# A fused lightning-attention and SwiGLU kernel: the first tile's outputs inside the third tile, five half buffers for the activations, and another order of groups 4 and 5

## The chip, the cores and the metric

The kernel runs on one core of one Trainium2 chip. The time is device microseconds of one execution; the number for a kernel is the median of several runs. Beside these runs stands one execution taken with the hardware profiler, whose rows are used below. In that core PE (TensorE) multiplies matrices into PSUM, DVE (VectorE), ACT (ScalarE) and POOL (GpSimd) work on tensors, and SP (SyncE) issues transfers. Each engine works through its own instructions in order and waits for semaphores that others raise.

## The reference

Attention over q, k and v of shape (4 batches, 8 heads, 768 positions, 64), in blocks of 64 positions, with a running state per batch and head that decays with lambda; its result, laid out as 3072 tokens by 512, goes through a gated feed-forward network.

```python
for b in range(nb):
    intra = einsum('bhic,bhjc->bhij', qb, kb) * Dmask
    intra = einsum('bhij,bhjd->bhid', intra, vb)
    inter = einsum('bhid,bhde->bhie', qb * lam_pow, kv_state)
    out[:, :, sl] = intra + inter
    kv_state = lam_block * kv_state + einsum('bhsd,bhse->bhde', kb * rev_pow, vb)
...
g = x @ w_gate            # 512 -> 1536
h = g * sigmoid(g) * (x @ w_val)
return h @ w_out          # 1536 -> 512
```

## The kernel before, in words

**Groups and tiles.** A group g is 256 positions of one batch in all heads; there are 12. Two groups make a tile t of 512 tokens, the unit of the feed-forward part; there are six. Groups 0 to 5 (`g < NAT0`) and groups 6 to 11 use different layouts of the same computation.

**Attention of one group.** `load_group` (L243) issues the loads of k, q and v on SP: three transfers, or ten for groups 6 and up. `cast_scaled` (L255) casts k on ACT and scales and casts q on DVE (L260), then `dma_transpose` (L248) issues one transposing transfer on SP (L251), which makes `qkt`. `v_scale` (L235) makes `v_s` on POOL (L238). `upd_mm` (L382) multiplies k by v for the state, `upd_copy` (L404) copies that on ACT to `ups`, and `state` (L421 to L432) is a chain of adds and casts on POOL that gives the states `kvn` and `kv`. `scores` (L326, or L352 for groups 6 and up) multiplies q by k; the masks on DVE (L333, L357) are put in a list, `later`, and taken from it by `run_later`. `core_a` multiplies q by the states (L461) into two PSUM banks and lets ACT read one element (`guard`, L445); `core_b` adds the product of masked scores and v (L474) and then evicts both banks to `xt` (L486), on ACT unless `SPLIT` gives one to DVE. `ahead(g)` is update, state and scores; `attend(g)` is `core_a(g)`, the update and scores of g + 1, and `core_b(g)`, in one visit.

**Feed-forward part.** `ffn_gate` (L514) multiplies by a 128-wide slice of w_gate and ACT takes Silu (L518); `ffn_val` (L528) does the same with w_val and DVE multiplies the two into `h` (L531). Such a pair is a step; a tile has 12. Tile 1's steps are cut in two halves: `s1a` for its first group, `s1b` for its second. `ffn_out(t, b)` (L547) then multiplies 128 tokens of `h` by all of w_out in 12 matmuls, ACT evicts (L549) and issues the store (L550). A tile's `h` is one buffer of [128, 12, 4, 128]; there are two.

**Output weights.** w_out comes in six transfers of 512 KB on SP (`wo_piece`, L227) and is cast by POOL, one piece by ACT (`wo_cast`, L232).

**PSUM.** All eight banks are handed out in turn by `bank()`: whatever asks for a bank gets the one that was handed out eight requests before.

**Order.** The order is written by hand. `at(n, fn, ...)` puts a call behind step n; the loop at L768 emits each step, one or two waiting masks, and then the calls of that step. In tile 1 this puts group 5's loads and all six weight pieces on SP behind s1a[3], the casts and the transposition of group 5 behind s1b[3], `ahead(4)` behind s1b[6], and at the end of the tile, behind s1b[11]:

```python
    at(s1b[11], ffn_out, 0, 0)
    at(s1b[11], ahead, 5)
    at(s1b[11], run_later, 3)
    at(s1b[11], ffn_out, 0, 1)
    at(s1b[11], core_a, 5)
    at(s1b[11], ffn_out, 0, 2)
    at(s1b[11], core_b, 5)
```

From tile 2 on, `sn[n]` are the steps of a tile, each of which carries the four outputs of the tile before it behind steps 0, 3, 7 and 9, the casts and loads of two groups, and two `attend` calls.

Of the kernel before, what the change touches and what calls it, by code (L numbers as in the profile page):

```python
# [9 lines left out]
BF16 = mybir.dt.bfloat16  # L10
# [27 lines left out]
def _body(ctx, tc, nc, q, k, v, lam, moe_w_gate, moe_w_val, moe_w_out, out):  # L38
# [5 lines left out]
    DFF = moe_w_gate.shape[1]  # L44
    MC = DM // 128
    FC = DFF // 128
    NG = NBLK * B // 2
    M = BLK // 2

# [17 lines left out]
    vs_pool = ctx.enter_context(tc.tile_pool(name="vs", bufs=4))  # L67
    ssb_pool = ctx.enter_context(tc.tile_pool(name="ssb", bufs=2))
    xt_pool = ctx.enter_context(tc.tile_pool(name="xt", bufs=2))
    h_pool = ctx.enter_context(tc.tile_pool(name="h", bufs=2))  # L70
    sil_pool = ctx.enter_context(tc.tile_pool(name="sil", bufs=3))
    osb_pool = ctx.enter_context(tc.tile_pool(name="osb", bufs=3))
    kv_pool = ctx.enter_context(tc.tile_pool(name="kv", bufs=1))
# [234 lines left out]
    def scores(g, cs=(0, 1), warm=0):  # L308
        if g >= NAT0:
            scores_n(g)  # L310
            return
        tt = st[("qkt", g)]
        sp = {(c, h2): bank() for c in cs for h2 in range(2)}
        warm_into(sp[(cs[0], 0)], warm)
        if ("ssb", g) not in st:
            st[("ssb", g)] = ssb_pool.tile([128, 2, HP, 2, BLK], BF16, name="ssb", tag="ssb")
        ssb = st[("ssb", g)]
        for c in cs:
            for hi in range(2):
                for s in range(2):  # L320
                    for b2 in range(2):
                        for h2 in range(2):
                            hp = 2 * c + hi
                            dp = slice(h2 * 64, h2 * 64 + 64)
                            n = (hi * 2 + s) * BLK
                            nc.tensor.matmul(  # L326
                                sp[(c, h2)][b2 * M:b2 * M + M, n:n + BLK],
                                tt[dp, 0, s, hp, b2 * M:b2 * M + M],
                                tt[dp, 1, :, hp, b2 * M:b2 * M + M],
                                start=True, stop=True, skip_group_check=True)  # L330
            for h2 in range(2):
                def do_mask(c=c, h2=h2):
                    nc.vector.tensor_tensor(  # L333
                        out=ssb[:, h2, 2 * c:2 * c + 2].rearrange("p a s n -> p a (s n)"),
                        in0=sp[(c, h2)].rearrange("p (a x) -> p a x", a=2),
                        in1=bap(causal, [[0, 2], [1, 2 * BLK]]),
                        op=ALU.mult)
                later.append(do_mask)
# [179 lines left out]
        nc.scalar.activation(sil[:, 0:N], gp[:, 0:N], AF.Silu)  # L518

    def ffn_val(t, fc, b0=0, b1=B):  # L520
        if ("h", t) not in st:
            st[("h", t)] = h_pool.tile([128, FC, B, BLK], BF16, name="h", tag="h")
        h_sb, xt, sil = st[("h", t)], st[("xt", t)], st[("sil", t, fc, b0)]
        N = (b1 - b0) * BLK
        fs = slice(fc * 128, fc * 128 + 128)
        vp = bank()
        for mc in range(MC):
            nc.tensor.matmul(vp[:, 0:N], wv_sb[:, mc, fs],  # L528
                             xt[:, b0 // 2:b1 // 2, mc].rearrange("p g b n -> p g (b n)"),
                             start=(mc == 0), stop=(mc == MC - 1))  # L530
        nc.vector.tensor_tensor(out=h_sb[:, fc, b0:b1].rearrange("p b n -> p (b n)"),  # L531
                                in0=sil[:, 0:N], in1=vp[:, 0:N], op=ALU.mult)

    def ffn_fc(t, fc, b0=0, b1=B):
# [1 line left out]
        ffn_val(t, fc, b0, b1)  # L536

    def ffn_out(t, b, last=False):
        h_sb = st[("h", t)]
        osb = osb_pool.tile([128, DM], FP32, name="osb", tag="osb")  # L540
        row = groups[2 * t + b // 2][0] * S + (groups[2 * t + b // 2][1] * 2 + b % 2) * BLK
        halves = ((0, DM // 2, nc.scalar.copy, nc.scalar), (DM // 2, DM, nc.vector.tensor_copy, nc.sync)) \
            if last else ((0, DM, nc.scalar.copy, nc.scalar),)
        for c0, c1, fn, eng in halves:
            ps = bank()[:, 0:c1 - c0]
            for fc in range(FC):
                nc.tensor.matmul(ps, h_sb[:, fc, b], wo_sb[:, fc, c0:c1],  # L547
                                 start=(fc == 0), stop=(fc == FC - 1))
            fn(out=osb[:, c0:c1], in_=ps)  # L549
            eng.dma_start(out=bass.AP(tensor=out.tensor, offset=out.offset + row * DM + c0,  # L550
                                      ap=[[DM, 128], [1, c1 - c0]]),
                          in_=osb[:, c0:c1])
# [3 lines left out]
        upd(g)  # L556
        scores(g)

    def attend(g):
        run_later(len(later))  # L560
        core_a(g)
        if g + 1 < NG:
            upd_mm(g + 1)
            upd_copy(g + 1)
            scores(g + 1)
            late, later[:] = later[:], []
        core_b(g)
        if g + 1 < NG:
            later[:] = late
            state(g + 1)  # L570
# [106 lines left out]
    def at(n, fn, *a):  # L677
        plan.setdefault(n, []).append((fn, a))
# [31 lines left out]
    s1b = [step(1, fc, 2, 4) for fc in range(FC)]  # L710
    at(s1a[3], cast_scaled, 4)
    at(s1a[3], load_group, 5)
    for c in range(0, FC, 2):
        at(s1a[3], wo_piece, c, c + 2)
    at(s1a[7], scores, 3, (0,))
    at(s1a[7], run_later, 2)
    at(s1a[8], scores, 3, (1,))
# [4 lines left out]
    at(s1a[10], core_b, 3, SPLIT)  # L722
    at(s1a[10], v_scale, 4, nc.gpsimd)
    at(s1a[10], state, 3)
    at(s1b[3], cast_scaled, 5)
    at(s1b[3], load_group, 6)
    at(s1b[4], wo_cast)
    at(s1b[4], wo_cast)
    at(s1b[6], ahead, 4)
    at(s1b[6], run_later, 2)  # L730
    at(s1b[6], wo_cast)
    at(s1b[6], wo_cast)
    at(s1b[6], v_scale, 5, nc.gpsimd)
    at(s1b[8], wo_cast)
    at(s1b[9], core_a, 4)
    at(s1b[10], core_b, 4)
    at(s1b[10], wo_cast, ACTC)
    at(s1b[11], ffn_out, 0, 0)
    at(s1b[11], ahead, 5)
    at(s1b[11], run_later, 3)  # L740
    at(s1b[11], ffn_out, 0, 1)
    at(s1b[11], core_a, 5)
    at(s1b[11], ffn_out, 0, 2)
    at(s1b[11], core_b, 5)
    at(s1b[11], cast_scaled, 6)
    at(s1b[11], load_group, 7)
    at(s1b[11], v_scale, 6, nc.gpsimd)
    at(s1b[11], ffn_out, 0, 3)

    outs = [(1, b) for b in range(4)]  # L750
    for t in range(2, NG // 2):
        sn = [step(t, fc) for fc in range(FC)]
        if t == 2:
            at(sn[2], ahead, 6)
        for j, g in ((3 if t == 2 else 0, 2 * t + 3), (7 if t == 2 else 6, 2 * t + 4)):
            if g < NG:
                at(sn[j], cast_scaled, g)
                if g + 1 < NG:
                    at(sn[j], load_group, g + 1)
                at(sn[1 + j], v_scale, g, nc.gpsimd)  # L760
        if t + 1 < NG // 2:
            at(sn[6 if t == 2 else 4], attend, 2 * t + 2)
            at(sn[10], attend, 2 * t + 3)
        for n, o in zip((0, 3, 7, 9), outs):
            at(sn[n], ffn_out, *o)
        outs = [(t, b) for b in range(4)]

    for n, (t, fc, b0, b1) in enumerate(steps):  # L768
        if t >= 1 and t + 1 < NG // 2 and ("xt", t + 1) not in st:
# [5 lines left out]
            if fn in (attend, ahead):  # L775
                run_later(1)
    run_later(len(later))
    for t, b in outs:
        ffn_out(t, b, last=(b == 3))
# [1 line left out]
_INS = ['q', 'k', 'v', 'lam', 'moe_w_gate', 'moe_w_val', 'moe_w_out']  # L781
_OUTS = [((3072, 512), 'float32')]
# [25 lines left out]
```

## Time and profile before

| | |
|---|---|
| median of 5 runs | 228.57 us (228.2 to 229.05) |
| profiled execution | 228.97 us |
| its span on the core | 227.3 us |
| PE busy | 219.5 us (97%), 2443 matmuls |
| ACT, DVE, POOL busy | 108.0 (48%), 90.0 (40%), 88.0 us (39%) |
| gate, value and output matmuls (L514, L528, L547) | 76.6, 76.4, 65.8 us |
| moved by DMA | 39.70 MB |

The span runs from the first to the last recorded instruction; the execution's own time also holds what lies around it. In the profile's rows the order is start, duration, engine, line, operation, out<-in and count; a bracket gives the idle time of the engine before the row and what ended it. PE's rows are matmuls, PEld's the weight loads beside them, a q behind an engine's name marks what its sequencer issues. Matmuls overlap, so a row of PE lasts longer than the time until the next one starts; distances between starts are the safer reading.

### The profile page before, as it was taken

To read this page: it belongs to the slowest core of one execution; us is meant where nothing else is said; L and a number is where in the kernel's file an instruction comes from. 1 tells how busy PE (TensorE), PEld (TensorE's weight loads), DVE (VectorE), ACT (ScalarE), POOL (GpSimd) and SP (SyncE) were. 2 spreads that over 40 slices of the span, in tenths; PEclk is the share of its full clock that TensorE was granted. 3 is DMA by queue.
4 is the path that set the end of the run, shared out by engine and by line. 5 is a ranking of instruction groups with operands and counts; after the bars stand their busy time and mean duration, and the time that the engine had idled before them with its cause. 6 is when DMAs were issued, how large, how long until landed. Compare 5 with 4: busy or idle time off the path is not lost.

```text
span 227.3 us, 5902 instructions
## 1 busy us (share of the span) xinstructions
PE 219.5 (97%) x2443; PEld 118.3 (52%) x2443; DVE 90.0 (40%) x151; ACT 108.0 (48%) x211; POOL 88.0 (39%) x130
## 2 busy tenths in 40 slices
PE   8889999999998999999999999999999999999994
PEld 3556455878863444454544544544544444444443
DVE  2664357685834213545353362253242123222200
ACT  6888585754662446354454463453433423322221
POOL 6576737542595222978363092092150000000000
PEclk9999999999999999999999999999999999999999
DMA  6999999899997878887888748915101101101122
GB/s 194 345 360 382 367 356 311 201 260 276 386 189 191 224 164 200 197 185 186 217 191 194 191 95 192 242 31 138 49 3 48 46 3 46 46 0 46 49 92 92
DMA packets 88012, 39.70 MB, mean 175 GB/s; under 512 B 57650, under 2 KB 83506, under 8 KB 87986
## 3 DMA queue, kind: packets, MB, share of 16 engines
q1 hardware_dynamic: 83474, 32.64, 54.8%
q10 hardware_dynamic: 4512, 6.69, 8.3%
q8 instruction: 19, 0.31, 0.6%
q14 instruction: 7, 0.06, 0.1%
HBM read 28.31 MB, written 6.29 MB: 152 GB/s over the span
## 4 chain that ended last, share of the span: by engine, by line
PE 83%; DMA 5%; SPq 4%; POOL 4%; ACT 1%; issue 1%; DVE 0%; DVEq 0%; POOLq 0%
PE bank L547 27%; PE bank L514 25%; PE bank L528 24%; DMA woraw<-in_moe_w_out_dram 3%; SPq L99 3%; DMA kraw<-in_k_dram 2%; PE bank L474 2%; POOL wo_sb L232 2%; PE bank L461 2%; PE bank L382 1%; PE bank L352 1%; POOL v_s L238 1%; PE bank L289 1%; PE bank L326 1%; SPq L227 1%
## 5 line engine op out<-in xcount | busy, mean ns | idle before, releaser
L531 DVE TENSOR_TENSOR h<-sil,bank 128x512 bf16<-128x512 bf16 (+1 forms) x87 | 51.4, 594 | 105.9 <-PE bank L528 86.7
L514 PE MATMUL bank<-xt,wg_sb 128*128 128x512 bf16 (+1 forms) x348 | 76.6, 343 | 0.0
L528 PE MATMUL bank<-xt,wv_sb 128*128 128x512 bf16 (+1 forms) x348 | 76.4, 342 | 0.0
L547 PE MATMUL bank<-wo_sb,h 128*128 128x512 bf16 (+1 forms) x300 | 65.8, 371 | 1.3 <-POOL wo_sb L232 1.3
L518 ACT ACTIVATE sil<-bank 128x512 bf16<-128x512 f32 (+1 forms) x87 | 45.9, 527 | 43.9 <-PE bank L514 40.9
L528 PEld LDWEIGHTS <-wv_sb 128*128 128x128 bf16 x348 | 34.0, 98 | 28.3
L547 PEld LDWEIGHTS <-h 128*128 128x128 bf16 x300 | 29.1, 98 | 33.8 <-issue 1.5
L514 PEld LDWEIGHTS <-wg_sb 128*128 128x128 bf16 x348 | 32.4, 98 | 27.2 <-DVE xt L486 0.3
L549 ACT COPY osb<-bank 128x512 f32<-128x512 f32 (+1 forms) x24 | 13.9, 578 | 54.5 <-PE bank L547 52.4
L238 POOL TENSOR_TENSOR v_s<-v,dec 128x1024 bf16<-128x1024 f32 (+1 forms) x14 | 23.2, 1666 | 16.8 <-DMA v<-in_v_dram 9.4
L421 POOL TENSOR_TENSOR kvf<-kvs,ups 128x256 f32<-128x256 f32 x8 | 5.8, 726 | 42.0 <-ACT ups L404 42.0
L333 DVE TENSOR_TENSOR ssb<-bank,causal 128x512 bf16<-128x512 f32 x24 | 15.3, 683 | 4.4 <-PE bank L326 4.3
L486 ACT CAST xt<-bank 128x512 bf16<-128x512 f32 x21 | 12.8, 663 | 2.9 <-PE bank L474 2.4
L430 POOL CAST kvn<-kvf 64x256 bf16<-64x256 f32 x24 | 12.5, 519 | 1.5
L421 POOL TENSOR_TENSOR kvf<-kvf,ups 128x256 f32<-128x256 f32 x16 | 11.6, 725 | 0.6
L260 DVE TENSOR_TENSOR qk<-qraw,qdn 128x1024 bf16<-128x1024 f32 x6 | 8.1, 1350 | 6.5 <-DMA qraw<-in_q_dram 6.5
L404 ACT COPY ups<-bank 128x256 f32<-128x256 f32 (+1 forms) x24 | 9.5, 450 | 2.4 <-PE bank L382 1.4
L258 ACT CAST qk<-kraw 128x1024 bf16<-128x1024 f32 x9 | 9.4, 1040 | 0.6 <-DMA kraw<-in_k_dram 0.6
L357 DVE TENSOR_TENSOR ssb<-bank,causaln 128x512 bf16<-128x512 f32 x12 | 8.2, 687 | 1.2 <-PE bank L352 1.0
L232 POOL CAST wo_sb<-woraw 128x1024 bf16<-128x1024 f32 x5 | 5.2, 1043 | 6.8 <-DMA woraw<-in_moe_w_out_dram 6.8
L221 POOL CAST wv_sb<-wraw 128x1024 bf16<-128x1024 f32 (+1 forms) x6 | 5.8, 970 | 5.0 <-DMA wraw<-in_moe_w_val_dram 4.9
L474 PE MATMUL bank<-ssb,v_s 64*64 64x128 bf16 (+1 forms) x384 | 7.0, 208 | 0.5 <-ACT guard L445 0.5
(65 smaller groups left out, 118.6 us busy)
## 6 DMA issues: line engine op xcount, KB each, us to landing
out_dram<-osb ACTq DMA_DIRECT2D x23, 256.0 KB, 2.2
v<-in_v_dram SPq DMA_DIRECT2D x16, 256.0 KB, 4.4
woraw<-in_moe_w_out_dram SPq DMA_DIRECT2D x6, 512.0 KB, 7.6
kraw<-in_k_dram SPq DMA_DIRECT2D x24, 128.0 KB, 3.4
qraw<-in_q_dram SPq DMA_DIRECT2D x24, 128.0 KB, 4.2
wraw<-in_moe_w_gate_dram SPq DMA_DIRECT2D x5, 512.0 KB, 6.7
wraw<-in_moe_w_val_dram SPq DMA_DIRECT2D x5, 512.0 KB, 7.7
kraw<-in_k_dram SPq DMA_DIRECT2D x4, 512.0 KB, 6.7
```

The lines of the kernel that those rows point to most:

```text
L238: eng.tensor_tensor(out=st[("vs", g)][:, h0:h1], in0=st[("v", g)][:, h0:h1].rearrange("p h (s d) -> p h s d", s=2), in1=vfac(g, h0, h1), o ...
L333: nc.vector.tensor_tensor(out=ssb[:, h2, 2 * c:2 * c + 2].rearrange("p a s n -> p a (s n)"), in0=sp[(c, h2)].rearrange("p (a x) -> p a x", ...
L421: nc.gpsimd.tensor_tensor(out=o, in0=f, in1=u, op=ALU.add)
L430: nc.gpsimd.tensor_copy(out=o[64 - h2 * 64:128 - h2 * 64], in_=f[h2 * 64:h2 * 64 + 64])
L474: nc.tensor.matmul(op[r][h2 * 64:h2 * 64 + 64, cols(g, hp, s)], v_s[ps, 2 * hp + h2, s], ssb[ps, h2, hp * 2 + s] if g >= NAT0 else ssb[ps, ...
L486: fns[r](out=xt[:, g % 2, :, r].rearrange("p h (m s) -> p h s m", s=2) if g < NAT0 else xt[:, g % 2, :, :, r * M:r * M + M], in_=op[r].rea ...
L514: nc.tensor.matmul(gp[:, 0:N], wg_sb[:, mc, fs], xt[:, b0 // 2:b1 // 2, mc].rearrange("p g b n -> p g (b n)"), start=(mc == 0), stop=(mc = ...
L518: nc.scalar.activation(sil[:, 0:N], gp[:, 0:N], AF.Silu)
L528: nc.tensor.matmul(vp[:, 0:N], wv_sb[:, mc, fs], xt[:, b0 // 2:b1 // 2, mc].rearrange("p g b n -> p g (b n)"), start=(mc == 0), stop=(mc = ...
L531: nc.vector.tensor_tensor(out=h_sb[:, fc, b0:b1].rearrange("p b n -> p (b n)"), in0=sil[:, 0:N], in1=vp[:, 0:N], op=ALU.mult)
L547: nc.tensor.matmul(ps, h_sb[:, fc, b], wo_sb[:, fc, c0:c1], start=(fc == 0), stop=(fc == FC - 1))
L549: fn(out=osb[:, c0:c1], in_=ps)
```

## The change

The `h` of a tile is cut into two half buffers of six slices each, and five such halves replace two whole buffers. Two of the six weight transfers stay behind s1a[3]; the other four are issued behind s1b[1], after the casts and the transposition of group 5, which move there from s1b[3]. `ahead(4)` moves to s1b[3], and `attend(4, (0,))` behind s1b[7] puts `core_a(4)`, the update of group 5, the first half of its scores and `core_b(4)` into one visit; the second half of the scores, `core_a(5)` and `core_b(5)` follow behind s1b[8], s1b[9] and s1b[10]. POOL does all six weight casts, two behind s1b[8] and four in tile 2. Tile 0's four outputs move from the end of tile 1 to sn[5] of tile 2, two on each side of `ahead(6)`; tile 1's outputs stand behind sn[6], sn[7], sn[9] and sn[10]; `attend(6)` moves from sn[6] to sn[8], and the casts and loads of tile 2 move accordingly. Tiles 3 to 5 keep their plan.

```diff
@@ -44,6 +44,7 @@
     DFF = moe_w_gate.shape[1]
     MC = DM // 128
     FC = DFF // 128
+    FH = FC // 2
     NG = NBLK * B // 2
     M = BLK // 2
 
@@ -67,7 +68,7 @@
     vs_pool = ctx.enter_context(tc.tile_pool(name="vs", bufs=4))
     ssb_pool = ctx.enter_context(tc.tile_pool(name="ssb", bufs=2))
     xt_pool = ctx.enter_context(tc.tile_pool(name="xt", bufs=2))
-    h_pool = ctx.enter_context(tc.tile_pool(name="h", bufs=2))
+    h_pool = ctx.enter_context(tc.tile_pool(name="h", bufs=5))
     sil_pool = ctx.enter_context(tc.tile_pool(name="sil", bufs=3))
     osb_pool = ctx.enter_context(tc.tile_pool(name="osb", bufs=3))
     kv_pool = ctx.enter_context(tc.tile_pool(name="kv", bufs=1))
@@ -518,9 +519,10 @@
         nc.scalar.activation(sil[:, 0:N], gp[:, 0:N], AF.Silu)
 
     def ffn_val(t, fc, b0=0, b1=B):
-        if ("h", t) not in st:
-            st[("h", t)] = h_pool.tile([128, FC, B, BLK], BF16, name="h", tag="h")
-        h_sb, xt, sil = st[("h", t)], st[("xt", t)], st[("sil", t, fc, b0)]
+        hn = ("h", t, fc // FH)
+        if hn not in st:
+            st[hn] = h_pool.tile([128, FH, B, BLK], BF16, name="h", tag="h")
+        h_sb, xt, sil = st[hn], st[("xt", t)], st[("sil", t, fc, b0)]
         N = (b1 - b0) * BLK
         fs = slice(fc * 128, fc * 128 + 128)
         vp = bank()
@@ -528,7 +530,7 @@
             nc.tensor.matmul(vp[:, 0:N], wv_sb[:, mc, fs],
                              xt[:, b0 // 2:b1 // 2, mc].rearrange("p g b n -> p g (b n)"),
                              start=(mc == 0), stop=(mc == MC - 1))
-        nc.vector.tensor_tensor(out=h_sb[:, fc, b0:b1].rearrange("p b n -> p (b n)"),
+        nc.vector.tensor_tensor(out=h_sb[:, fc % FH, b0:b1].rearrange("p b n -> p (b n)"),
                                 in0=sil[:, 0:N], in1=vp[:, 0:N], op=ALU.mult)
 
     def ffn_fc(t, fc, b0=0, b1=B):
@@ -536,7 +538,6 @@
         ffn_val(t, fc, b0, b1)
 
     def ffn_out(t, b, last=False):
-        h_sb = st[("h", t)]
         osb = osb_pool.tile([128, DM], FP32, name="osb", tag="osb")
         row = groups[2 * t + b // 2][0] * S + (groups[2 * t + b // 2][1] * 2 + b % 2) * BLK
         halves = ((0, DM // 2, nc.scalar.copy, nc.scalar), (DM // 2, DM, nc.vector.tensor_copy, nc.sync)) \
@@ -544,7 +545,7 @@
         for c0, c1, fn, eng in halves:
             ps = bank()[:, 0:c1 - c0]
             for fc in range(FC):
-                nc.tensor.matmul(ps, h_sb[:, fc, b], wo_sb[:, fc, c0:c1],
+                nc.tensor.matmul(ps, st[("h", t, fc // FH)][:, fc % FH, b], wo_sb[:, fc, c0:c1],
                                  start=(fc == 0), stop=(fc == FC - 1))
             fn(out=osb[:, c0:c1], in_=ps)
             eng.dma_start(out=bass.AP(tensor=out.tensor, offset=out.offset + row * DM + c0,
@@ -556,13 +557,13 @@
         upd(g)
         scores(g)
 
-    def attend(g):
+    def attend(g, cs=(0, 1)):
         run_later(len(later))
         core_a(g)
         if g + 1 < NG:
             upd_mm(g + 1)
             upd_copy(g + 1)
-            scores(g + 1)
+            scores(g + 1, cs)
             late, later[:] = later[:], []
         core_b(g)
         if g + 1 < NG:
@@ -710,8 +711,8 @@
     s1b = [step(1, fc, 2, 4) for fc in range(FC)]
     at(s1a[3], cast_scaled, 4)
     at(s1a[3], load_group, 5)
-    for c in range(0, FC, 2):
-        at(s1a[3], wo_piece, c, c + 2)
+    at(s1a[3], wo_piece, 0, 2)
+    at(s1a[3], wo_piece, 2, 4)
     at(s1a[7], scores, 3, (0,))
     at(s1a[7], run_later, 2)
     at(s1a[8], scores, 3, (1,))
@@ -722,48 +723,51 @@
     at(s1a[10], core_b, 3, SPLIT)
     at(s1a[10], v_scale, 4, nc.gpsimd)
     at(s1a[10], state, 3)
-    at(s1b[3], cast_scaled, 5)
-    at(s1b[3], load_group, 6)
-    at(s1b[4], wo_cast)
-    at(s1b[4], wo_cast)
-    at(s1b[6], ahead, 4)
-    at(s1b[6], run_later, 2)
-    at(s1b[6], wo_cast)
-    at(s1b[6], wo_cast)
-    at(s1b[6], v_scale, 5, nc.gpsimd)
+    at(s1b[1], cast_scaled, 5)
+    for c in range(4, FC, 2):
+        at(s1b[1], wo_piece, c, c + 2)
+    at(s1b[1], v_scale, 5, nc.gpsimd)
+    at(s1b[1], load_group, 6)
+    at(s1b[3], ahead, 4)
+    at(s1b[3], run_later, 2)
+    at(s1b[7], attend, 4, (0,))
+    at(s1b[8], scores, 5, (1,))
+    at(s1b[8], run_later, 2)
     at(s1b[8], wo_cast)
-    at(s1b[9], core_a, 4)
-    at(s1b[10], core_b, 4)
-    at(s1b[10], wo_cast, ACTC)
-    at(s1b[11], ffn_out, 0, 0)
-    at(s1b[11], ahead, 5)
-    at(s1b[11], run_later, 3)
-    at(s1b[11], ffn_out, 0, 1)
-    at(s1b[11], core_a, 5)
-    at(s1b[11], ffn_out, 0, 2)
-    at(s1b[11], core_b, 5)
-    at(s1b[11], cast_scaled, 6)
-    at(s1b[11], load_group, 7)
-    at(s1b[11], v_scale, 6, nc.gpsimd)
-    at(s1b[11], ffn_out, 0, 3)
-
-    outs = [(1, b) for b in range(4)]
+    at(s1b[8], wo_cast)
+    at(s1b[9], core_a, 5)
+    at(s1b[10], core_b, 5, SPLIT)
+
     for t in range(2, NG // 2):
         sn = [step(t, fc) for fc in range(FC)]
         if t == 2:
-            at(sn[2], ahead, 6)
-        for j, g in ((3 if t == 2 else 0, 2 * t + 3), (7 if t == 2 else 6, 2 * t + 4)):
+            for n in range(4):
+                at(sn[n], wo_cast)
+            at(sn[4], cast_scaled, 6)
+            at(sn[4], load_group, 7)
+            at(sn[4], v_scale, 6, nc.gpsimd)
+            at(sn[5], ffn_out, 0, 0)
+            at(sn[5], ffn_out, 0, 1)
+            at(sn[5], ahead, 6)
+            at(sn[5], ffn_out, 0, 2)
+            at(sn[5], ffn_out, 0, 3)
+        for j, g in ((6 if t == 2 else 0, 2 * t + 3), (9 if t == 2 else 6, 2 * t + 4)):
             if g < NG:
                 at(sn[j], cast_scaled, g)
                 if g + 1 < NG:
                     at(sn[j], load_group, g + 1)
-                at(sn[1 + j], v_scale, g, nc.gpsimd)
-        if t + 1 < NG // 2:
-            at(sn[6 if t == 2 else 4], attend, 2 * t + 2)
+                if t > 2:
+                    at(sn[1 + j], v_scale, g, nc.gpsimd)
+                else:
+                    at(sn[j], v_scale, g, nc.gpsimd)
+        if t > 2 and t + 1 < NG // 2:
+            at(sn[4], attend, 2 * t + 2)
             at(sn[10], attend, 2 * t + 3)
-        for n, o in zip((0, 3, 7, 9), outs):
-            at(sn[n], ffn_out, *o)
-        outs = [(t, b) for b in range(4)]
+        for n, b in zip((6, 7, 9, 10) if t == 2 else (0, 3, 7, 9), range(4)):
+            at(sn[n], ffn_out, t - 1, b)
+        if t == 2:
+            at(sn[8], attend, 6)
+            at(sn[10], attend, 7)
 
     for n, (t, fc, b0, b1) in enumerate(steps):
         if t >= 1 and t + 1 < NG // 2 and ("xt", t + 1) not in st:
@@ -775,8 +779,8 @@
             if fn in (attend, ahead):
                 run_later(1)
     run_later(len(later))
-    for t, b in outs:
-        ffn_out(t, b, last=(b == 3))
+    for b in range(4):
+        ffn_out(NG // 2 - 1, b, last=(b == 3))
 # ---- launch: one core; inputs and outputs as the reference has them ----
 _INS = ['q', 'k', 'v', 'lam', 'moe_w_gate', 'moe_w_val', 'moe_w_out']
 _OUTS = [((3072, 512), 'float32')]
```

## The prediction

> **What bounds the kernel now.** I read the busy shares first, then the table of windows, then the chain of waits, then TensorE's rows in time order. TensorE (PE) is busy 97% of the span at full clock, no other engine over 48%. The windows table (columns: window, its length, then busy us and count of PE, weight loads, DVE, ACT, POOL) says where PE is not busy once it is running:
>
> ```profile
> 40.00:66.00 26.00, 26.00 (x413) 21.60 (x412) 17.63 (x36) 15.00 (x38) 13.32 (x17) 1.00 0.99 268
> 66.00:80.00 14.00, 12.73 (x163) 6.18 (x161) 4.13 (x6) 6.32 (x13) 6.67 (x9) 1.00 0.79 199
> 80.00:113.00 33.00, 33.00 (x447) 16.21 (x446) 13.22 (x17) 15.46 (x28) 18.48 (x25) 1.00 0.82 193
> ```
>
> Between 40 and 113 us, where every edit lies, PE idles once, by 14.00 − 12.73 = 1.27 us. Its timeline shows the place:
>
> ```profile
> 66.08 1.89 PE L547 MATMUL bank<-wo_sb,h 128*128 128x512 bf16 x8
> 69.24 1.02 PE L547 MATMUL bank<-wo_sb,h 128*128 128x512 bf16 x4 [1.27 <-POOL wo_sb L232]
> ```
>
> The first output of tile 0 issues 8 of 12 matmuls and waits for the cast of the last output-weight piece. Matmuls issue 0.216 us apart (12 in 2.59 us), so the eighth's slot ends at 66.08 + 1.73 = 67.81 and **1.43 us** of issue time are lost (the shown idle is shorter because of the pipeline's tail). The chain of waits leads back through POOL's casts to the weight transfers on SP's queue. So the most that this stage gives is 1.43 us plus whatever attention costs less; whatever makes PE wait elsewhere is added whole.
>
> Below, "step" is one gate+value pair: 0.87 us (half width, tile 1) or 1.73 us (full); an output is 2.59 us. s1b[n] are tile 1's second-half steps, sn[n] those of tile 2. All PE starts are issue times of the timeline.
>
> **1. The outputs move into tile 2: −1.43.** Nothing is removed: 12×4 output matmuls, 4 evictions and 4 stores stay. Their first use goes from 66.1 to after sn[5], which by the sums below is about 79.5. The weights: four pieces are issued after group 5's transposition, which lands at 62.3 (part 3); before, six pieces landed 1.25 us apart, so the last is there by about 68. POOL runs state(5) until 66, then six casts of 1.04: done by about 72. Margin 7 us: the wait goes, and no ACT cast is needed. The half buffers of h: the fifth is fresh for tile 2's first half; its second half reuses tile 0's first, whose last reader is ahead of it in PE's own order. No wait. The outputs of tile 1 then run in the same tile as before, so the tail is unchanged.
>
> **2. Groups 4 and 5 merged: −0.16.** Visits to attention cost, from one L528's end to the next L514's or L547's start: ahead(4) 59.40→60.33 = 0.93, core_a(4) 0.70, core_b(4) 0.67, ahead(5) 70.10→71.02 = 0.92, core_a(5) 0.67, core_b(5) 0.68; sum 4.57. After: ahead(4) 0.93; one visit core_a(4), upd_mm(5), half of scores(5), core_b(4) = 0.10 + 0.46 + 0.27 + 0.25 + 0.58 = 1.66 (each piece from its row's start to the next row's start); the other half of scores(5) 0.45 (as 47.43→47.88); core_a(5) 0.70; core_b(5) 0.67; sum 4.41.
>
> **3. Group 5's transposition: +0.27.** Its casts move from s1b[3] to s1b[1]. q5 landed at 54.93; DVE's cast can start behind the s1b[1] product at 55.65 and takes 1.22, so the transposition issues at 57.0, not 58.75. SP's rows:
>
> ```profile
> 48.96 2.93 SPq L99 DMA_DIRECT2D v<-in_v_dram  x1
> 51.93 4.44 SPq L227 DMA_DIRECT2D woraw<-in_moe_w_out_dram  x6
> 58.75 7.56 SPq L251 DMA_TRANSPOSE qkt<-qk  x1
> ```
>
> Only two weight pieces stay ahead of it; the second landed at 60.28. When is the transposition needed? s1b[4] to s1b[7] follow ahead(4): PE 56.78 + 0.93 + 4×0.87 = 61.19; scores(5) starts 0.10 + 0.46 + 0.27 later, at 62.03. **Rule against row.** The median transposition lands 4.0 us after issue: 61.0, no wait. "DMA: Bandwidth & Descriptors", section "Queues, rings and completion order", of the Trainium skill, says that each DMA engine takes a queue's descriptors in ring order, so it cannot overtake the two pieces. The completion records fit the rule: group 4's transposition ended at 49.61, 2.04 after the v load queued ahead (47.57). By the rule 60.28 + 2.04 = 62.3, a wait of 0.27. I take that; ends 0 and 1.7 (rival B).
> Queued behind on SP are four weight pieces and group 6's ten loads; they have the margin of part 1, and group 6 is now used at sn[4]. Behind the earlier casts of group 5, ACT's Silu and DVE's product of s1b[2] end at 57.2; ahead(4) writes their bank at 57.4. v_scale(5) now stands ahead of state(4) on POOL: v5 landed at 56.44, so it ends at 58.4 (58.8 beside DVE's cast), state(4)'s first kvn at 60.0, and core_a(4) reads it at 61.3. These covers are 0.2 and 1.3 us and cost nothing unless gone; then their excess is PE's.
>
> **4. Bank reuse after the merged visit: +0.50, +0.13.** The second half of scores(5) is written to the two PSUM banks that core_b(4) has just filled; ACT evicts these one after the other. Before, the same eviction:
>
> ```profile
> 64.62 0.64 PE L474 MATMUL bank<-ssb,v_s 64*64 64x128 bf16 x32
> 65.20 0.61 PE L514 MATMUL bank<-xt,wg_sb 128*128 128x256 bf16 x4
> ...
> 65.32 1.33 ACT L486 CAST xt<-bank 128x512 bf16<-128x512 f32 x2 [0.58 <-PE bank L474]
> ```
>
> (The last row is ACT's.) From E, the start of the next gate, the second bank is free at 66.65 − 65.20 = 1.45, plus 0.05 for the semaphore (69.19→69.24 above). PE needs it at E + 0.87 + 0.10 + 0.02: it waits **0.50**. Before, a step and an output lay between this eviction and the banks' reuse. Behind it: ACT's Silu of s1b[8] comes after both evictions (done E+1.85), DVE's product after that (E+2.3), and the next mask, queued behind the product, at E+2.9; core_a(5) wants that bank at E+2.8: 0.13.
>
> **5. Into tile 2: +0.06.** One half step (0.87) covers the eviction of group 5, as after group 3 at 52.35: evictions done 53.23, next gate 53.28, that is 0.93 for 0.87. Before, a whole output covered it.
>
> **6. Tile 2's attention comes later and closer: +0.50.** attend(6) moves from sn[6] to sn[8]; attend(7) stays at sn[10]. POOL's queue decides. In before:
>
> ```profile
> 99.90 0.72 POOL L421 TENSOR_TENSOR kvf<-kvs,ups 128x256 f32<-128x256 f32 x1 [1.47 <-ACT ups L404]
> ...
> 105.97 1.27 POOL L425 CAST kv<-kvs 128x256 bf16<-128x256 f32 x1
> 108.13 1.91 POOL L238 TENSOR_TENSOR v_s<-v,dec 128x1024 bf16<-128x1024 f32 x1 [0.89 <-DMA v<-in_v_dram]
> ```
>
> state(7) starts 1.71 us after attend(6) (98.19) and ends at +9.05; v_scale(8) is queued behind it and is needed by attend(7)'s upd_mm(8). Now: v_scale(8) ends at 9.05 + 1.91 = +10.96, plus 0.05. PE's need: attend(6) 1.49, step, output, step, output = 10.13, plus 0.36 (111.78→112.14) = +10.49. Wait **0.5**; before, v_scale ended 2.1 us ahead.
> **Rule against row.** The last cast took 1.27 instead of its usual 0.40, beside a DVE cast of q (L260) of 1.66 instead of 1.22. "SBUF — State Buffer", section "Who interferes with whom", of the Trainium skill, says why: a DVE operation with two SBUF inputs and a GpSimd one that reads SBUF exclude each other. The moved cast of q8 falls into state(7) again (about +5.3), so by the rule the 0.87 stays; had it been chance, v_scale would end 0.4 early and the wait be 0. I keep the row; ends 0 and 1.0.
> The transposition of group 8 is as close: SP issues 7's transposition and 8's ten loads (7.2 us of issuing) from 3.0 us after sn[6]; q8 lands at about +5.2, its cast ends +6.8, the transposition lands at +10.9; scores(8) wants it at +10.8, or +11.3 with the wait above. It adds nothing if loading is not late.
> ahead(6) at sn[5] is covered: its transposition lands 6.5 us after sn[4], two outputs and a step put the need at 7.3. Two of group 7's loads now wait for the completion of tile 0's first outputs (shared semaphores): about 1 us late, with 2 to spare. Group 9's loads, moved from sn[7] to sn[9], land at about +17.5, hold DVE's cast at tile 3's first step for 1 us, and its transposition lands at +23 for a need at +27.6.
>
> **Sum.** −1.43 − 0.16 + 0.27 + 0.50 + 0.13 + 0.06 + 0.50 = **−0.13 us**. The profiled execution took 228.97 (span 227.3 and 1.7 around it), so 228.84; it lies 0.40 above the median of 228.57, so the median should be **228.4**.
>
> **Rivals.** A, the close calls hold: transposition in time, v_scale(8) early; only parts 4 and 5 cost. −1.59 + 0.69 = −0.9: **227.7**. For it: 62.03 against 62.3 and 0.5 of 11 us are within a trace's scatter. Against: both sums use rows of this trace without any allowance.
> B, slower: the transposition lags behind a slow DMA engine. In before it landed at 69.90, 3.4 us after the last weight piece (55.50 + 11.0 = 66.47). With 3.4 for 2.04 it lands at 63.7 and scores(5) waits 1.7: −0.13 + 1.4 = +1.3: **229.9**. It decides against the change from a landing later than about 62.4. For it: that one row; against: the transposition of group 4.
> C: group 8's loads are 1 us late, as single loads in the trace are; its transposition passes the v_scale wait by 0.6 to 1.2: **229.4**.
> That the change fails to remove the weight wait would need casts 7 us late; I give it nothing.
>
> **How the numbers follow.** Forecast 0.40, A 0.29, B 0.20, C 0.11. A measurement here tells 0.2%, 0.46 us, from no change. The forecast lies within that, A is faster, B and C slower: 0.29, 0.40, 0.31. The range runs from 227.4 (A with 0.3 of scatter) to 229.8, leaving most of B's upper half out.
>
> **What would show it.** PE's 1.27 idle on the weight cast gone; PE waiting about 0.3 at the first L327 (old L326) of group 5 for the transposition, 0.5 at the second for ACT's xt eviction, 0.5 at upd_mm(8) for POOL's v_s; tile 3's first gate within 0.5 us of the old 114.91 (113.18 + 1.73), since the same work stands ahead of it. Wrong if PE waits at an output, in tile 3 or later, or if one of the three waits exceeds 1 us.

## The result, and the profile after

| | before | after |
|---|---|---|
| median | 228.57 us (39 runs) | 229.56 us (20 runs, 229.06 to 230.62 and one of 232.52) |
| ratio after to before | | 1.0045, interval 1.0031 to 1.0058 |
| profiled execution, span | 228.97, 227.3 us | 229.32, 227.6 us |
| first gate of s1b[0] to first gate of tile 3 | 53.28 to 114.91 = 61.63 us | 53.05 to 115.26 = 62.21 us |

The changed kernel is slower by 0.3 to 0.6%. Here and below, medians are of all runs, while ratios and their intervals leave out the few runs in a slower state, more than 1.5% above the fastest of their kernel, such as the one of 232.52. The stretch in the last row holds every edit and grew by 0.58 us; the prediction had −0.13.

The windows view of the changed kernel, cut as before (window, its length, then busy us and count of PE, weight loads, DVE, ACT, POOL; last PE's granted clock, the DMA share and GB/s):

```profile
40.00:66.00 26.00, 25.73 (x476) 21.08 (x475) 18.52 (x38) 15.51 (x39) 16.13 (x20) 1.00 1.00 282
66.00:80.00 14.00, 13.80 (x102) 7.01 (x101) 7.41 (x12) 6.04 (x11) 7.40 (x7) 1.00 0.54 124
80.00:113.00 33.00, 32.02 (x399) 15.47 (x399) 10.19 (x12) 13.30 (x24) 16.52 (x24) 1.00 0.81 204
```

The 1.27 us of idle PE that stood in the middle window are gone. In their place there are 0.27, 0.20 and 0.98 in the three windows: one wait has become four small ones. PE's timeline shows the first two, and the last two further on (line numbers are one or two higher than before):

```profile
61.79 0.42 PE L327 MATMUL bank<-qkt 64*64 64x128 bf16 x16
62.03 0.63 PE L475 MATMUL bank<-ssb,v_s 64*64 64x128 bf16 x32
...
63.57 0.24 PE L327 MATMUL bank<-qkt 64*64 64x128 bf16 x1
64.08 0.41 PE L327 MATMUL bank<-qkt 64*64 64x128 bf16 x15 [0.27 <-ACT xt L487]
...
66.95 0.30 PE L475 MATMUL bank<-ssb,v_s 64*64 64x128 bf16 x7
67.46 0.55 PE L475 MATMUL bank<-ssb,v_s 64*64 64x128 bf16 x25 [0.20 <-issue]
...
112.17 0.44 PE L383 MATMUL bank<-v_s,qk 64*64 64x64 bf16 x24 [0.74 <-POOL v_s L239]
112.85 0.45 PE L353 MATMUL bank<-qkt 64*64 64x64 bf16 x32 [0.24 <-DMA qkt<-qk]
```

The transposition of group 5 was in time: no wait at 61.79. At 64.08 the forecast wait for the eviction stands, 63.57 to 64.08 = 0.51 us. At 67.46 PE pauses inside core_b(5), with no semaphore behind it. At 112.17 and 112.85 attend(7) waits twice.

Since matmul rows overlap, what a visit to attention costs is better read from the end of the last feed-forward slot to the next feed-forward start. In these terms, for the profiled execution and two further profiles of each kernel (`b1_before`, `b2_before`, `c1_after`, `c2_after`; us):

| | before | after |
|---|---|---|
| wait for the weight cast | 1.43, 0.59, 1.66 | none |
| visits of groups 4 and 5, pause left out | 4.53, 4.73, 4.53 | 4.81, 4.84, 5.05 |
| pause in core_b(5) | none | 0.41, 0.70, 0.21 |
| ahead(6), attend(6) | 2.25, 2.24, 2.25 | 2.29, 2.33, 2.33 |
| attend(7) | 1.40, 1.41, 1.41 | 2.63, 1.84, 1.84 |
| s1b[0] to tile 3 | 61.63, 61.00, 61.88 | 62.21, 61.77, 61.50 |

> Before's kernel unchanged, for a second profile of it. Theory: one wait of about 1.4 us at the first output for the cast of a weight piece and no other between 40 and 113 us; 61.6 us from s1b[0] to tile 3, within 0.3. If that wait varies by as much as the others do, before's stage is as loose as after's.

> The kernel before, unchanged, looked at a third time for the scatter of its waits. If the weight wait varies with the execution, it lies again between 0.5 and 1.5 us; if the first look (1.43) was typical and the second (0.59) chance, it lies near 1.4. Theory: it varies.

> After's kernel unchanged, for a second profile of it. Theory (the new waits are races whose size differs from one execution to the next): the time from s1b[0]'s first gate to tile 3's first gate again above before's 61.63 us, by 0.5 to 1.5; the transposition's wait at scores(5), the pause inside core_b(5) and the wait at attend(7) each between 0 and 1.3 us. Rival (they are fixed): 62.21 us as in the first profile, with the same waits within 0.1.

> The changed kernel, unchanged, looked at a third time for the scatter of its waits. Theory: the pause inside core_b(5) stands again at the same instruction with 0.2 to 1.0 us, the half scores of group 5 wait about 0.5 us for the eviction, and attend(7) loses between 0.4 and 1.3 us, more where the cast of q7 took 2.9 us and less where it took 1.2 us.

So nearly every term moves from execution to execution, the removed wait most of all: `b1_before` was expected to show about 1.4 us of it and showed 0.59. It has the same row as the prediction's, with a third of its idle time:

```profile
68.32 1.02 PE L547 MATMUL bank<-wo_sb,h 128*128 128x512 bf16 x4 [0.42 <-POOL wo_sb L232]
```

In the mean of three profiles the stretch from s1b[0] to tile 3 is 0.32 us longer, by the medians the kernel is 0.99 longer: the profiled executions of the changed kernel (229.32, 228.87 and 228.85 us) all lie below its median, two of the three of the kernel before (228.97, 228.26, 228.98) above. The experiments' medians have to carry what the profiles can't.

### The profile page after: what moved, and what is told of

The parts are those of the page before. It is cut to its first block, busy times and chain, and to the rows that moved or that the text cites. A ratio compares the mean times of both kernels' runs of the same rounds, so it can differ in the third digit from the quotient of the medians.

```text
span 227.6 us, 5905 instructions
## 1 busy us (share of the span) xinstructions
PE 218.7 (96%) x2443; PEld 117.9 (52%) x2443; DVE 91.4 (40%) x152; ACT 106.4 (47%) x209; POOL 89.2 (39%) x131
## 4 chain that ended last, share of the span: by engine, by line
PE 85%; DMA 5%; SPq 4%; ACT 2%; issue 1%; DVE 1%; DVEq 0%
PE bank L515 27%; PE bank L530 26%; PE bank L548 24%; SPq L107 2%; DMA kraw<-in_k_dram 2%; PE bank L475 2%; DMA qkt<-qk 2%; PE bank L462 2%; DMA qraw<-in_q_dram 1%; PE bank L327 1%; PE bank L383 1%; SPq L100 1%; PE bank L290 1%; SPq L252 1%; PE bank L353 1%
## 5 line engine op out<-in xcount | busy, mean ns | idle before, releaser
L239 POOL TENSOR_TENSOR v_s<-v,dec 128x1024 bf16<-128x1024 f32 (+1 forms) x14 | 24.3, 1739 | 21.6 <-DMA v<-in_v_dram 18.3
L487 ACT CAST xt<-bank 128x512 bf16<-128x512 f32 x20 | 12.2, 659 | 2.9 <-PE bank L475 2.8
L431 POOL CAST kvn<-kvf 64x256 bf16<-64x256 f32 x24 | 11.6, 483 | 1.5
L261 DVE TENSOR_TENSOR qk<-qraw,qdn 128x1024 bf16<-128x1024 f32 x6 | 9.0, 1506 | 4.1 <-DMA qraw<-in_q_dram 4.1
L475 PE MATMUL bank<-ssb,v_s 64*64 64x128 bf16 (+1 forms) x384 | 6.9, 207 | 0.7 <-ACT guard L446 0.5
L475 PEld LDWEIGHTS <-v_s 64*64 64x64 bf16 x384 | 5.4, 105 | 2.3 <-issue 2.1
```

The source lines that it names most:

```text
L239: eng.tensor_tensor(out=st[("vs", g)][:, h0:h1], in0=st[("v", g)][:, h0:h1].rearrange("p h (s d) -> p h s d", s=2), in1=vfac(g, h0, h1), o ...
L431: nc.gpsimd.tensor_copy(out=o[64 - h2 * 64:128 - h2 * 64], in_=f[h2 * 64:h2 * 64 + 64])
L475: nc.tensor.matmul(op[r][h2 * 64:h2 * 64 + 64, cols(g, hp, s)], v_s[ps, 2 * hp + h2, s], ssb[ps, h2, hp * 2 + s] if g >= NAT0 else ssb[ps, ...
L487: fns[r](out=xt[:, g % 2, :, r].rearrange("p h (m s) -> p h s m", s=2) if g < NAT0 else xt[:, g % 2, :, :, r * M:r * M + M], in_=op[r].rea ...
```

## The experiments

Expectations stand as they were written before each run. Times are medians; ratios are to the kernel before.

### The wait for the two banks taken away

```diff
-    def attend(g, cs=(0, 1)):
+    def attend(g, cs=(0, 1), fns=(nc.scalar.copy, nc.scalar.copy)):
...
-        core_b(g)
+        core_b(g, fns)
...
-    at(s1b[7], attend, 4, (0,))
+    at(s1b[7], attend, 4, (0,), SPLIT)
```

> After's kernel, but group 4's two banks are evicted side by side (DVE and ACT) in the merged visit. Theory (each new PE wait is added whole to the time): the 0.51 us wait of scores(5)'s second half for ACT's eviction goes, nothing takes its place; 0.5 us below after's kernel, ratio to before 1.002 instead of 1.0045. Rival (the masks and core_b(5) behind it wait anyway, the time comes back there): no change, 1.0045.

Measured: 229.86 us, ratio 1.0053 (1.0035 to 1.0071). The wait at the second half of the scores went (0.44 us for 0.95), and nothing was gained. PE's timeline shows a new wait in the merged visit:

```profile
62.74 0.36 PE L327 MATMUL bank<-qkt 64*64 64x128 bf16 x12 [0.80 <-ACT ups L405]
```

The named releaser isn't the cause: in the profile after, the same matmuls started at 61.79 while these copies to `ups` ended at 62.74. What landed at 62.70 is the transposition of group 5; the visit took 2.58 us for 1.61. It landed between 60.88 and 62.70 in seven profiles of kernels with the same queue up to there, for a need at about 61.8.

### v_scale(7) off POOL

In the profile after, group 7's cast on DVE and its v_scale on POOL begin together. DVE, POOL and SP's queue:

```profile
93.56 2.93 DVE L261 TENSOR_TENSOR qk<-qraw,qdn 128x1024 bf16<-128x1024 f32 x1
```

```profile
93.50 1.91 POOL L239 TENSOR_TENSOR v_s<-v,dec 128x1024 bf16<-128x1024 f32 x1 [0.69 <-DMA v<-in_v_dram]
...
110.21 1.91 POOL L239 TENSOR_TENSOR v_s<-v,dec 128x1024 bf16<-128x1024 f32 x1 [0.38 <-DMA v<-in_v_dram]
```

```profile
96.64 1.64 SPq L252 DMA_TRANSPOSE qkt<-qk  x1
```

The cast, usually 1.22 us, took 2.93; the transposition was issued at 96.64 and, behind it on SP, all of group 8's loads. v8 landed at 110.1, so that POOL waited 0.38 for it and v_scale(8) ended at 112.12: the 0.74 of PE. q8's lateness is the 0.24 behind it. Before, v_scale(7) stood behind the state chain and ran long after the cast. DVE, then POOL, in the profile before:

```profile
92.33 1.56 DVE L260 TENSOR_TENSOR qk<-qraw,qdn 128x1024 bf16<-128x1024 f32 x1 [0.36 <-DMA qraw<-in_q_dram]
```

```profile
96.52 1.91 POOL L238 TENSOR_TENSOR v_s<-v,dec 128x1024 bf16<-128x1024 f32 x1
```

```diff
-                    at(sn[j], v_scale, g, nc.gpsimd)
+                    at(sn[j], v_scale, g, nc.vector if g == 7 else nc.gpsimd)
```

> After's kernel, but v_scale(7) runs on DVE behind the cast of q7 instead of on POOL beside it. Theory (v_scale(7) and the cast of q7 exclude each other, so the cast takes 2.93 us, the transposition of group 7 and all of group 8's loads behind it on SP are some 1.6 us late, and v8 and group 8's transposition end PE's waits at attend(7)): the cast takes 1.2 to 1.3 us, group 7's transposition issues about 1.6 us earlier after sn[6], attend(7) takes about 1.9 us instead of 2.63; 0.7 us below after's kernel, ratio 1.0014. Rival (POOL's state(7) chain alone holds v_scale(8), loading plays no part): attend(7) stays at 2.6, ratio 1.0045.

Measured: 229.79 us, 1.0062 (1.0040 to 1.0083). The mechanism is as the theory had it: the cast took 1.21, the transposition was issued at 95.66, attend(7) took 1.93. But the pause in core_b(5) was 0.87 us in this profile, and the median didn't fall: what the clash is worth in the median is not shown, and six runs could not tell a few tenths. `c2_after` shows that the clash isn't in every execution either. DVE, then POOL:

```profile
93.84 1.22 DVE L261 TENSOR_TENSOR qk<-qraw,qdn 128x1024 bf16<-128x1024 f32 x1
```

```profile
95.85 1.91 POOL L239 TENSOR_TENSOR v_s<-v,dec 128x1024 bf16<-128x1024 f32 x1 [2.78 <-DMA v<-in_v_dram]
```

Here v7 landed 2 us later, the two didn't meet, and attend(7) took 1.84: 0.44 over before, for a forecast of 0.50.

### Group 8 loaded earlier

```diff
+            at(sn[5], load_group, 8, "kq")
...
-                    at(sn[j], load_group, g + 1)
+                    at(sn[j], load_group, g + 1, "v" if g == 7 else "kqv")
```

> After's kernel, but k and q of group 8 are loaded behind tile 0's outputs, ahead of group 7's transposition; v of group 8 stays behind it. Theory of late loads: the cast of q7 still takes about 2.9 us, but q8 is there 6 us before its cast and v8 about 4 us earlier than in after's kernel, so only POOL's queue (state(7), then v_scale(8)) is left: attend(7) about 1.9 us instead of 2.63, ratio 1.0014. Rival (POOL alone): 2.6, ratio 1.0045. If the transposition of group 7 is pushed back by the earlier loads, attend(6) shows it (over 1.53 us).

> After's kernel with the side-by-side eviction of the first run, k, q and v of group 8 loaded ahead of group 7's transposition, and v_scale(8) ahead of state(7) on POOL. Theory: no wait is left at attend(7) (1.40 us) nor at scores(5); 1.7 us below after's kernel, 0.7 below before's: ratio 0.997. Rival (one of the two waits only moves): above 1.000.

`e4_both` adds SPLIT, v8 ahead of group 7's loads and v_scale(8) at sn[7]. Measured: 236.23 us, 1.0298 (1.0259 to 1.0336), and 236.39, 1.0366 (1.0343 to 1.0389): both far off the theory. In `e3_kq8_early` SP's queue held the eight loads from 90.47 to 98.6, so that group 7's transposition was issued at 98.72 instead of 94.7 to 96.6, and landed at 106.1, 7.4 us later, where other profiles have 3.7 to 5.1. PE, and the windows after the wait:

```profile
106.16 0.64 PE L353 MATMUL bank<-qkt 64*64 64x64 bf16 x32 [4.72 <-DMA qkt<-qk]
106.61 0.62 PE L475 MATMUL bank<-ssb,v_s 64*64 64x64 bf16 x32
107.16 1.89 PE L515 MATMUL bank<-xt,wg_sb 128*128 128x512 bf16 x4
```

```profile
107.60:111.40 3.80, 3.58 (x10) 1.33 (x9) 0.54 (x1) 2.29 (x4) 2.92 (x3) 0.50 0.19 42
111.40:115.00 3.60, 3.60 (x17) 1.66 (x17) 1.88 (x3) 0.66 (x2) 0.00 (x0) 0.97 0.11 26
```

After 4.7 us without work PE's granted clock was 0.50 (third column from the end): the gate at 107.16 lasts 1.89 us instead of 1.04. The runs don't answer the question that they were made for; they show that eight loads ahead of that transposition cost far more than they could save.

### The weights issued late, or just behind the transposition

In six profiles the pause in core_b(5) stood before the same matmul (the eighth of L475). It ended 2.2 to 2.5 us after a 16 KB transfer on an instruction queue began: begun 64.97, matmul 67.46 in the profile after; 65.37 and 67.75 in `c1_after`; 65.41 and 67.73 in `c2_after`; 65.72 and 68.19 in `e2_vs7_dve`; 65.13 and 67.35 in `e6_wo_behind` (below); 66.20 and 68.68 in `e4_both`. Pieces of w_out land around that time, in the profile after at 62.81, 65.58 and 69.07. The profile doesn't say whose instructions a transfer carries; that they are PE's is read from this fixed distance.

```diff
-    at(s1a[3], wo_piece, 0, 2)
-    at(s1a[3], wo_piece, 2, 4)
...
-    for c in range(4, FC, 2):
-        at(s1b[1], wo_piece, c, c + 2)
...
     at(s1b[8], scores, 5, (1,))
     at(s1b[8], run_later, 2)
+    for c in range(0, FC, 2):
+        at(s1b[8], wo_piece, c, c + 2)
```

> After's kernel, but all six output-weight pieces are issued behind s1b[8], after group 5's transposition and group 6's loads; they are needed only at sn[5]. Theory (group 5's transposition waits for the pieces queued ahead of it, and the 16 KB instruction transfer whose end PE awaits inside core_b(5) starts late because the weight pieces fill the DMA engines): the transposition lands 3.9 to 4.1 us after issue in every execution, the pause in core_b(5) is gone; 0.5 us below after's kernel, ratio 1.002. Rival (the pause comes from how densely PE's instructions follow each other, not from the DMA engines): the pause stays, ratio 1.0045 or 0.2 us below it.

Measured: 228.95 us, 1.0004 (0.9982 to 1.0026), the first version below the changed kernel, by 0.6 us. The instruction transfer began at 63.30 and the pause is gone, with PE's instructions as dense as before. PE:

```profile
66.61 0.60 PE L530 MATMUL bank<-xt,wv_sb 128*128 128x256 bf16 x4
67.14 0.64 PE L475 MATMUL bank<-ssb,v_s 64*64 64x128 bf16 x32
```

The 32 matmuls of core_b(5) run through. The transfer itself takes 0.88 to 0.98 us with the weights and without; it is its start that moves. From the start of the merged visit to the start of the transfer it is 3.2 to 4.5 us in the eight profiles of versions with early weights, 2.2 and 2.6 in the two with late ones. The two profiles with early weights and no pause fit: in `e1_split` and `e3_kq8_early` it began 3.5 and 2.6 us ahead of that matmul. The edit also takes the pieces from ahead of the transposition, which landed at 60.58. To part the two, `e6_wo_behind` issues all six pieces behind s1b[1], behind the transposition, so that they are still in the engines when the instruction transfer comes:

```diff
-    at(s1a[3], wo_piece, 0, 2)
-    at(s1a[3], wo_piece, 2, 4)
...
-    for c in range(4, FC, 2):
+    for c in range(0, FC, 2):
         at(s1b[1], wo_piece, c, c + 2)
```

> The changed kernel with the two output-weight pieces that stood ahead of group 5's transposition issued behind it: all six pieces behind s1b[1], none behind s1a[3]. The transposition now has no weight piece ahead of it, but the DMA engines still work on weights between 58 and 69 us, when the 16 KB instruction transfer comes. It parts the two things that the late weights (at s1b[8]) took away together. Theory 1 (the instruction block behind the weights is what the late weights saved): the transposition lands at 60.5 and never binds, the pause inside core_b(5) stays at 0.2 to 1.2 us or grows, and the median stays at 229.4 to 229.7. Theory 2 (the wait for the transposition, 0 to 1 us from execution to execution, is what they saved): the median falls to 228.9 to 229.1, as with the late weights.

Measured: 229.83 us, 1.0050 (1.0030 to 1.0071). The transposition landed at 60.49 and never bound, and nothing was gained: theory 1. The pause was 0.30 in its profile, which is not more than before; more was lost there at attend(7):

```profile
113.28 0.45 PE L353 MATMUL bank<-qkt 64*64 64x64 bf16 x32 [1.28 <-DMA qkt<-qk]
```

attend(7) took 3.21 us, though group 7's transposition was issued early, at 94.87. The last load of q8 landed at 107.67, where `c2_after` had it at 106.13, and group 8's transposition at 113.24. So group 8 can be late without the clash of the two engines. Over eight profiles of versions of the changed kernel (`e3_kq8_early` and `e4_both` left out), attend(7) lost 0.44 three times, 0.49, 0.53, 1.14, 1.23 and 1.81 us: the 0.44 is the floor that v_scale(8), or in one case another wait of the same length, sets.

In the medians the versions part by the place of the weights: with early weights 1.0045 (the changed kernel), 1.0053, 1.0062 and 1.0050, with late ones 1.0004 and, in the next section, 0.9986.

### The three repairs together

SPLIT, the late weights, and v_scale(7) and (8) on DVE:

> After's kernel with the side-by-side eviction, late weight pieces as in the run before, and v_scale(7) and v_scale(8) on DVE behind the casts of q. Theory: no bank wait, no wait at attend(7) (1.4 us instead of 2.63), no transposition wait; 2 us below after's kernel, 1 us below before's: ratio 0.996. Rival (dense instructions): the pause in core_b(5) grows to 0.8 to 1.2 as it did without the bank wait, ratio 0.999 to 1.000.

Measured: 228.68 us, 0.9986 (0.9960 to 1.0012): 0.9 us below the changed kernel, and not told apart from the kernel before, nor from the late weights alone. The theory had 0.996. Visits of groups 4 and 5 took 4.43 us, with no pause; attend(7) still took 1.84.

### The removed wait by itself

Could the kernel before lose its wait without the rest? POOL's last cast stood behind v_scale(5). One line moves:

```diff
+    at(s1b[3], v_scale, 5, nc.gpsimd)
     at(s1b[4], wo_cast)
     at(s1b[4], wo_cast)
...
-    at(s1b[6], v_scale, 5, nc.gpsimd)
```

> The kernel before with one line moved: v_scale(5) on POOL stands behind s1b[3], ahead of the first output-weight cast, instead of behind the fourth. It asks what the weight wait alone was worth, with nothing else of the change. Theory (the -1.43 term of the prediction is an upper end): POOL's last cast ends about 67.4 instead of 69.2 and the weight wait is gone; the transposition of group 5 lands at 69.7 to 69.9 as in both looks at the kernel before, the first matmul of scores(5) wants it about 0.7 after the first output's last slot, at 69.4 to 69.5, so 0.3 to 0.5 of the gain is taken back; the time falls by 0.3 to 1.0 us, to 227.6 to 228.3. Rival (the weight wait is worth its whole 1.43): 227.1 with no wait at scores(5). Second rival (the wait of PE only moves): no change, 228.6.

Measured: 227.63 us, 0.9961 (0.9949 to 0.9973), below both kernels. POOL, then PE:

```profile
64.95 3.01 POOL L232 CAST wo_sb<-woraw 128x1024 bf16<-128x1024 f32 x3
```

```profile
66.37 2.75 PE L547 MATMUL bank<-wo_sb,h 128*128 128x512 bf16 x12
69.06 0.45 PE L382 MATMUL bank<-v_s,qk 64*64 64x64 bf16 x32
69.99 0.64 PE L326 MATMUL bank<-qkt 64*64 64x128 bf16 x32 [0.49 <-DMA qkt<-qk]
```

The casts end at 67.96 instead of 69.19 and the output's 12 matmuls run through. In the profile of the kernel before, the wait for the weights covered the next lateness; here it shows: the transposition of group 5 landed at 69.95, and the visit took 1.60 for 0.92. (Another 0.26 stands inside scores(4), with no releaser named.) This execution, 228.53 us, is the longest of the kernel's 22 runs. In the median the wait alone was worth 0.94 us.

## Why the prediction was wrong

The forecast was no change, 228.4 us, 0.17 below the kernel before; the time was 229.56, 0.99 above it and inside the range. Two steps carry most of the 1.16 us between: part 1 was mis-sized, −0.94 for −1.43, and what the early weights cost, 0.6 to 0.7 us in the median, by what looks like a stop of PE for an instruction block, stands in no part. A clause of part 6 failed too, in some executions. The other new waits came, and in sum near their forecast size.

**Part 1, −1.43: mis-sized.** The wait went as described: six casts on POOL, no wait at any output. But 1.43 was one execution's number; it lies between 0.59 and 1.66, and removing it alone brought 0.94 in the median (`d1_before_v5`), with part of it taken back by the transposition in the one profile of it. The 0.40 by which the profiled execution lay above its median was then subtracted as well, though it was probably a part of this same wait: the three profiled executions less their own waits are 227.54, 227.67 and 227.32 us, about the 227.63 of the kernel that lost the wait alone. An execution without the wait has no such excess to give back; without that step the same sum reads 228.84, and the 0.72 to the measured time is about what the early weights cost.

**Not in the prediction: the pause.** The change puts the attention of groups 4 and 5, with its many short matmuls (96 in the merged visit of 1.6 us), into the time in which the weights are moved, and an instruction block comes late: 0.21 to 1.27 us in six of eight profiles of versions with the early weights, nothing in the two with the late ones. The prediction weighed the new place of the weights only against POOL's casts and the transposition. That the dense matmuls are needed for it as well is not tested.

**Parts 2, 4 and 5: right, but for the mask.** The merged visit took 1.61 for a forecast of 1.66; the bank wait 0.51, 0.53 and 0.53 for 0.50; the step into tile 2 cost 0.92 for 0.93. The mask's 0.13 didn't come (core_a(5) took its 0.66).

**Part 3, +0.27: the rule was right, the row under it moved.** The transposition landed 1.96 us after the weight piece queued ahead (58.92 to 60.88), as the ring-order rule and group 4's row had it (2.04); over seven profiles it was 1.8 to 2.0. But that piece landed at 58.92 and not at 60.28, and from profile to profile the wait was 0, 0, 0.22 and, in `e1_split`, 0.96. Rival B's row is no accident either: behind all six pieces, in the kernel before and `d1_before_v5`, it was 3.4 in four profiles; why is not shown. The wait decides little: `e6_wo_behind` takes the pieces away from ahead of the transposition and is no faster.

**Part 6, +0.50: right in its size, with one clause that failed.** The v_scale(8) wait is there: attend(7) lost 0.44 in two of three profiles, and in the profile after state(7) ended 9.12 us after the start of attend(6) for a forecast of 9.05. What failed is "It adds nothing if loading is not late". Loading was late, in the profile after by the clash of v_scale(7) with the cast of q7, elsewhere by the loads alone, and attend(7) then lost 0.7 to 1.4 above the 0.44, in three profiles of eight. The prediction weighed the shared-port rule at q8's cast and didn't ask it of v_scale(7), which the change moved from behind the state chain to a POOL that idles until v7 lands, at the very time of q7's cast. Rival C had such a price (0.6 to 1.2), with a chance of 0.11. That its 229.4 lies nearest to the measured time is luck: it starts from the mis-sized −1.43, has no pause, and only one of the three profiles of the changed kernel shows its lateness.

**The sum.** By the profiles, means of three: the wait −1.23, the pause +0.44, groups 4 and 5 otherwise +0.30 (forecast +0.74), the step into tile 2 +0.05 (+0.06), ahead(6) and attend(6) +0.07 (0), attend(7) +0.70 (+0.50): together +0.33, where the stretch grew by 0.32. In the medians: the wait −0.94; the weights that meet the instruction transfer +0.61, the changed kernel less `e5_wo_late`, or +0.74 with each against the kernel before measured beside it; with the +1.12 of the other terms this gives 0.8 to 0.9 of the measured 0.99.

**What stays open.** That early weights cost this in the median is shown by `e5_wo_late`, and `e6_wo_behind` speaks against the transposition ahead of which they stood, unless its attend(7) is worse in the median too, which one profile can't tell. Group 6's loads, which `e5_wo_late` puts ahead of the weights, were late in neither (ahead(6) took 0.75 and 0.81). That the cost is the instruction block rests on the pause, which goes with the late weights, and on the fixed distance to the transfer; but the pause in the profile of `e6_wo_behind` is small, and no profile caught an execution of the changed kernel above its median, so where those spend their time is not known.

**The signs.** In the profile after, the signs named in advance nearly all came out: no wait for the weights, none for the transposition (forecast 0.27), 0.51 at the banks, 0.74 at upd_mm(8), no more idle PE from 113 to 215 us than before (101.73 us busy in both), and tile 3's first gate at 115.26, within 0.5 of 114.91. That last sign was blunt: s1b[0] had started 0.23 us earlier than before, which hid part of the 0.58.

## What to carry to other kernels

A wait read from one execution is a draw: before a change is built to remove it, profile two or three executions, and ask what is late next behind it (here one moved line took 0.94 us). Where a profiled execution lies above the median, the wait that is to go may be the excess; don't subtract it twice. The new waits of this change could be calculated to a few tenths of a microsecond; what the sum lacked was a resource that nobody had listed. When an operation or a transfer is moved, ask of every engine that shares a port with it, and of the instruction supply, what else will run at its new time.

## What was not expected of the hardware

**Instruction supply is visible.** The Trainium skill, "Runtime: NRT & Kernel Launch", section "Instruction fetch mechanics", has the refill in 16 KiB blocks as mostly hidden. The profile here lists 19 transfers and 0.31 MB on the instruction queue, 16 KB each, and in six profiles PE stopped for 0.2 to 1.3 us at a fixed instruction, 2.2 to 2.5 us after one of them began. The profile names such a stop only "issue".

**Who starts second pays.** q7's cast began 0.06 us after v_scale(7) in the profile after and took 2.93 instead of 1.22. In `c1_after` the cast began first, v_scale took 2.89 instead of 1.91, and the transposition was issued 1.4 us earlier. DVE, then POOL:

```profile
93.86 1.21 DVE L261 TENSOR_TENSOR qk<-qraw,qdn 128x1024 bf16<-128x1024 f32 x1
```

```profile
93.96 2.89 POOL L239 TENSOR_TENSOR v_s<-v,dec 128x1024 bf16<-128x1024 f32 x1 [0.86 <-DMA v<-in_v_dram]
```

The Trainium skill, "SBUF — State Buffer", section "Who interferes with whom", calls the port pair that DVE and GpSimd share an exclusive lock and says that issue order decides who blocks; these rows agree, and show that a landing time, 93.4 or 93.9, decides which engine is held up. The move in `d1_before_v5` made the same clash: v_scale(5) began at 56.59 and the cast of q5, 0.87 us behind it, took 2.12. It cost nothing there, since the transposition had six weight pieces ahead of it.

**An idle PE comes back at half clock.** In `e3_kq8_early` PE waited 4.72 us, to 106.16; the granted clock was 0.90 in the window from 104 to 105, 0.50 from 105 to 111, and 1.00 again from 112. By the two ratios that kernel took 5.8 us more than the changed one, with the wait itself.
